# Fewer products in a linear-attention backward pass, and other buffers at the entrance of a softmax core

## Chip, cores and metric

One core of one Trainium2 chip. The metric is the device time of one execution in microseconds (us), lower is better. The kernel before takes 1096.92 us (median of 3 runs, 1093.32 to 1097.35). All runs told here are of the fast state; differences are called faster or slower only above 2%, so most of what follows is about effects below that line, and rests on profiles and on many runs.

Engines have the profiler's names: PE is TensorE's matrix products, PEld its weight loads, ACT is ScalarE, DVE VectorE, POOL GpSimd, SP SyncE; a q behind a name (SPq) marks the issue of a transfer. The granted clock is the share of TensorE's full clock that a throttle let through; a run's "clock" is its mean over the run.

## The reference, cut to what matters

Forward and backward (a vector-Jacobian product) of two attention blocks on 2048 tokens of 448 features with 16 heads of 28: A is linear attention, B is softmax attention with one shared k and v.

```python
phi = lambda t: jnp.where(t > 0, t + 1, jnp.exp(t)) + 1e-6
kv  = einsum("bhsd,bhse->bhde", phi(k), v);  z = einsum("bhsd->bhd", phi(k))
o_A = einsum("bhqd,bhde->bhqe", phi(q), kv) / (einsum("bhqd,bhd->bhq", phi(q), z) + 1e-6)
o_B = softmax(q k^T / sqrt(28)) v          # k, v shared by the 16 heads
out = concat([o_A @ wo_A, o_B @ wo_B]);    # returned with the gradients of all inputs
```

## The kernel before

It has three stages: A (linear attention, to about 200 us), the projections of B (to about 228 us), and the core of B, a loop of 512 units, each of two 128x512 tiles of scores, with its backward part 16 units behind (so "unit 16" is the first in which all engines work). The parts that matter:

```python
# awk: ring of 3 buffers per name. "osb" serves the outputs of A and the spread 1/den alike
def den_rx(q4, todo):
    for s in todo:
        rx = awk.tile([P, 512], BF16, name="osb")[:, 0:D]
        nc.scalar.activation(out=rx..., in_=rden[:, st, :]...to_broadcast([P, H, DH]), func=ACT.Copy)
        nc.vector.tensor_tensor(out=pq[:, st, 0:D], in0=pq[:, st, 0:D], in1=rx, op=ALU.mult)
        nc.vector.tensor_tensor(out=wq_n[:, st, 0:D], in0=wq_n[:, st, 0:D], in1=rx, op=ALU.mult)
def outA(st):
    ...                                        # 4 products into ps
    ot = awk.tile([P, 512], BF16, name="osb")[:, 0:D]
    nc.scalar.activation(out=ot[:], in_=ps[:, :], func=ACT.Copy)
    nc.scalar.dma_start(out0[st * P:(st + 1) * P, 0:D], ot[:])
# ... gradient of x of A: 3 x 4 products for each of the 16 token tiles
for st in range(NS):
    for tT_, w_ in [(pkT, VWT), (gqT, wqT), (gkT, wkT)]:
        for k in range(4):
            mm(ps[:, :], tT_[:, st, k, :], w_[:, k, :], start=(n == 0), stop=(n == 11))
# ... B: q by tokens (qn, 16 KB of each partition) is made by DMA transposes and written to memory
nc.sync.dma_start(qn_d[q2, :].rearrange(...), qn[:, t2, :])          # two writes of 1 MB
# v and k by tokens: 128 products of 32 columns
for w, dst in [(1, vaug_), (0, kn_)]:
    for st in range(NS):
        for c in range(4):
            mm(ps[:, st, :], xbT[:, c, st * P:(st + 1) * P], rep[:, w, c, 0:32], ...)
    nc.vector.tensor_copy(out=dst, in_=ps[:])
# core: the pools are stacked on memory that stage A and qn used
px_ = tile_pool(name="cdsx", bufs=2); pq_ = tile_pool(name="cqX", bufs=2)
pc_ = tile_pool(name="ccp", bufs=3);  pw_ = tile_pool(name="cwk", bufs=4)
```

## Time and profile before

| window of the profile before (us) | what it is | PE busy | granted clock |
|---|---|---|---|
| 62 to 110 | A: its outputs and gradients by token tile | 45.6 of 48.0 | 1.00 |
| 110 to 224 | A's weight and input gradients, B's projections | 113.8 of 114.0 | 1.00 |
| 224 to 229 | border to the core | 4.0 of 5.0 | 1.00 |
| 229 to 243 | entrance of the core, PE at half clock | 13.5 of 14.0 | 0.51 |
| 254 to 1047 | core | 758 of 793 | 1.00 |

The lines behind this table are in the prediction. Three more lines are needed later: rl (the reciprocals of the softmax sums, the core's first small tile) and the load of qX (q for the core), both behind the second write of q, and the first product with the backward scores, where unit 16 begins (timeline of the kernel before; columns: start, length, engine, line, operation, out<-in, shape, count; in brackets the idle time before it and what ended it).

```profile
246.59 0.18 DVE L762 RECIPROCAL rl<-sps 128x4 f32<-128x4 f32 x1 [0.86 <-DMA qn_d<-gaT]
247.08 1.16 POOL L878 DMA_DIRECT2D qX<-qn_d  x2 [18.66 <-PE dps L80]
254.08 0.69 DVE L870 TENSOR_TENSOR dsT<-dps,eT 128x512 bf16<-128x512 f32 x1
```

### The profile page before, as it was taken

The numbers are of one execution on the slowest core, as the hardware profiler recorded it, in microseconds if no ns is written. First come the engines' busy times: TensorE is split into PE (matmuls) and PEld (weight loads), VectorE is DVE, ScalarE is ACT, GpSimd is POOL, SyncE is SP. The second block draws the span as 40 slices with busy tenths as digits, with TensorE's granted clock in tenths as the row PEclk, the third lists the DMA queues.
The fourth block names the chain that finished last, engine by engine and source line by source line (L and its number), as shares of the span: only waits on it lengthen the run. The fifth ranks groups of instructions, "written<-read, shape, count | busy, mean of one in ns | idle before, by whom it ended". The sixth has DMA issues, their size and how long they took to land.

```text
span 1093.6 us, 38651 instructions
## 1 busy us (share of the span) xinstructions
PE 1047.3 (96%) x15645; PEld 489.8 (45%) x15645; DVE 896.3 (82%) x1772; ACT 876.1 (80%) x1744; POOL 758.1 (69%) x986
## 2 busy tenths in 40 slices
PE   9999999999999999999999999999999999999998
PEld 5545555444444444444444444444444444444444
DVE  7887400427999999999999999999999999999842
ACT  6453122468999999999999999999999999999521
POOL 6001242226888888888888888988988898888740
PEclk9999999979999999999999999999999999999999
DMA  9969899299999999999999999999999999999962
GB/s 264 153 126 173 172 173 213 61 200 224 183 209 173 174 190 187 197 181 192 196 179 195 193 196 185 196 196 172 198 192 196 185 193 188 192 180 178 221 139 63
DMA packets 668338, 198.96 MB, mean 182 GB/s; under 512 B 645392, under 2 KB 664128, under 8 KB 668160
## 3 DMA queue, kind: packets, MB, share of 16 engines
q1 hardware_dynamic: 656320, 175.18, 93.6%
q0 software_dynamic: 6880, 17.37, 6.3%
q10 hardware_dynamic: 4960, 3.96, 1.3%
q8 instruction: 122, 2.00, 0.7%
q14 instruction: 56, 0.46, 0.1%
HBM read 21.00 MB, written 12.94 MB: 31 GB/s over the span
## 4 chain that ended last, share of the span: by engine, by line
PE 35%; POOL 26%; ACT 23%; issue 10%; DVE 3%; DMA 1%; POOLq 0%; ACTq 0%; DVEq 0%
POOL dsT L873 22%; ACT cp L872 13%; PE agen L80 13%; ACT eT L903 9%; PE aacc L80 5%; PE sps L80 4%; PE oq L633 4%; PE sps L633 3%; PE dps L80 2%; PE dv_acc L633 2%; PE dk_acc L633 1%; PE dps L633 1%; DMA out_dram<-osb 1%; POOL prod L767 1%; POOL don L770 1%
## 5 line engine op out<-in xcount | busy, mean ns | idle before, releaser
L873 POOL TENSOR_TENSOR dsT<-cp,eT 128x512 bf16<-128x512 bf16 x512 | 588.4, 1157 | 103.9 <-ACT cp L872 96.4
L934 DVE STREAM_TRANSPOSE dsx<-dsT 128x512 f32<-128x512 f32 x512 | 357.6, 699 | 2.0
L870 DVE TENSOR_TENSOR dsT<-dps,eT 128x512 bf16<-128x512 f32 x512 | 342.3, 668 | 16.5 <-PE dps L633 9.1
L865 ACT ACTIVATE eT<-sps 128x512 bf16<-128x512 f32 x512 | 312.5, 610 | 27.5 <-PE dps L633 12.9
L633 PEld LDWEIGHTS <-R 32*128 32x128 bf16 (+1 forms) x8192 | 203.1, 93 | 281.9 <-issue 254.4
L872 ACT ACTIVATE cp<-dps 128x512 bf16<-128x512 f32 x512 | 314.1, 614 | 11.6 <-PE dps L633 9.3
L903 ACT ACTIVATE eT<-sps 128x512 bf16<-128x512 f32 x512 | 320.3, 626 | 0.0
L633 PE MATMUL dk_acc<-dsx,qX 32*32 32x512 bf16 x4096 | 268.0, 375 | 0.0
L633 PE MATMUL dps<-doT,R 32*128 32x256 bf16 x2048 | 248.9, 269 | 12.9 <-DVE dsT L870 7.5
L633 PE MATMUL sps<-R,R 32*128 32x256 bf16 x2048 | 218.7, 275 | 2.6 <-DVE oTs L763 0.8
L633 PE MATMUL oq<-eT,R 128*32 128x256 bf16 x2048 | 158.5, 276 | 0.0
L633 PE MATMUL oq<-dsT,R 128*32 128x256 bf16 x2048 | 157.2, 275 | 0.1
L633 PEld LDWEIGHTS <-qX 32*32 32x32 bf16 x4096 | 79.7, 89 | 114.7 <-issue 53.9
L633 PE MATMUL dv_acc<-eN,don 128*32 128x512 bf16 x1024 | 108.7, 379 | 0.0
L80 PEld LDWEIGHTS <-R 128*128 128x128 bf16 (+1 forms) x673 | 57.6, 99 | 55.8 <-issue 24.8
L396 POOL MEMSET ga<- 64x448 bf16 x2 | 0.9, 472 | 94.4 <-DVE pr L347 81.4
L546 DVE TENSOR_TENSOR osb<-R 32x512 bf16<-32x512 bf16 x4 | 1.6, 412 | 62.3 <-ACT R L543 62.3
L633 PEld LDWEIGHTS <-don 128*32 128x32 bf16 x1024 | 33.8, 97 | 0.7 <-issue 0.2
L888 DVE TENSOR_SCALAR R<-oq 64x256 bf16<-64x256 f32 x64 | 27.3, 427 | 4.6 <-PE oq L633 2.6
L878 POOL DMA_DIRECT2D qX<-qn_d x32 | 18.1, 570 | 18.7 <-PE dps L80 18.7
L80 PE MATMUL agen<-R,R 128*128 128x448 bf16 x128 | 28.6, 352 | 0.5 <-DVE pq L234 0.3
L499 ACT ACTIVATE wdq<-agen 128x448 bf16<-128x448 f32 x16 | 8.7, 543 | 25.1 <-PE agen L80 25.1
(219 smaller groups left out, 1012.4 us busy)
## 6 DMA issues: line engine op xcount, KB each, us to landing
qX<-qn_d POOLq DMA_DIRECT2D x32, 256.0 KB, 4.6
out_dram<-osb ACTq DMA_DIRECT2D x22, 112.0 KB
qn_d<-gaT SPq DMA_DIRECT2D x2, 1024.0 KB
eN<-eT SPq DMA_TRANSPOSE x128
xa<-in_A_x_dram SPq DMA_DIRECT2D x8, 224.0 KB
ga<-in_grad_out_dram SPq DMA_DIRECT2D x4, 448.0 KB
xa<-in_grad_out_dram POOLq DMA_DIRECT2D x4, 448.0 KB, 8.8
out_dram<-wdq POOLq DMA_DIRECT2D x8, 224.0 KB, 4.5
```

The source lines that it names most:

```text
L80: nc.tensor.matmul(out_ap, lhsT=lhsT, rhs=rhs, start=start, stop=stop, tile_position=(0, 0))
L633: nc.tensor.matmul(out, lhsT=lhsT, rhs=rhs, start=start, stop=stop, tile_position=pos, skip_group_check=True)
L767: nc.gpsimd.tensor_tensor(out=prod[b][:], in0=dnv, in1=os_, op=ALU.mult)
L770: nc.gpsimd.tensor_tensor(out=dn[:], in0=dnv, in1=r_[:].to_broadcast([P, 2, 2, 32]), op=ALU.mult)
L865: nc.scalar.activation(out=eT(u)[:, 0, :], in_=sp[0][:, :], func=ACT.Exp, scale=scale)
L870: nc.vector.tensor_tensor(out=dst[:, 0, :], in0=dp[0][:, :], in1=ew[:, 0, :], op=ALU.mult)
L872: nc.scalar.activation(out=cp[:, :], in_=dp[1][:, :], func=ACT.Copy)
L873: nc.gpsimd.tensor_tensor(out=dst[:, 1, :], in0=cp[:, :], in1=ew[:, 1, :], op=ALU.mult)
L878: nc.gpsimd.dma_start(qX[qc][32 * a:32 * a + 32, :, :, :].rearrange("j b s c -> j b (s c)"), qn_d[qc * 256:(qc + 1) * 256, :].rearrange("( ...
L888: nc.vector.tensor_scalar(out=qT_B[g][64 * hp:64 * hp + 64, qc * 256:(qc + 1) * 256], in0=oq[64:128, 0:256], scalar1=scale, scalar2=None, ...
L903: nc.scalar.activation(out=eT(u)[:, 1, :], in_=sp[1][:, :], func=ACT.Exp, scale=scale)
L934: nc.vector.transpose(out=dsx[b][:, tp, :, :, :].rearrange("p h t c -> p (h t c)").bitcast(F32), in_=dsT[y][:, :, :].rearrange("p h c -> p ...
```

## The change

Four parts. (1) The spread 1/den leaves the ring "osb", which output transfers hold, for the ring "phiT". (2) The last 64 features of q's gradient are put into the unused half of pk's last chunk, so eleven products do what twelve did. (3) v and k by tokens are picked out of rows already projected, by a selection matrix: 32 narrow products for 128. (4) The core's pools are stacked in another order, to take its first tiles off the memory of q by tokens.

```diff
 # 1
-                rx = awk.tile([P, 512], BF16, name="osb")[:, 0:D]
+                rx = awk.tile([P, D], BF16, name="phiT")[:, :]
 # 2
         for q4 in range(4):
+            t4 = slice(4 * q4, 4 * q4 + 4)
+            nc.gpsimd.tensor_copy(out=pk[:, t4, D:512], in_=gqn[:, t4, 3 * P:D])
             dma_T(pkT, pk, 4 * q4, 4)
@@
         prod_to(VWT, dkvT_blk, wvT, False)
+        nc.gpsimd.dma_start(VWT[64:128, 3, :], wqT[0:64, 3, :])
@@
-            for tT_, w_ in [(pkT, VWT), (gqT, wqT), (gkT, wkT)]:
-                for k in range(4):
-                    mm(..., start=(n == 0), stop=(n == 11))
+            for tT_, w_, nk in [(pkT, VWT, 4), (gqT, wqT, 3), (gkT, wkT, 4)]:
+                for k in range(nk):
+                    mm(..., start=(n == 0), stop=(n == 10))
 # 3
+        sel = cA.tile([P, 32], BF16, name="sel")          # identity without its first row
@@
-        for w, dst in [(1, vaug_), (0, kn_)]:
+        for rows, dst in [(vT, vaug_), (kT, kn_)]:
             for st in range(NS):
-                for c in range(4):
-                    mm(ps[:, st, :], xbT[:, c, st * P:(st + 1) * P], rep[:, w, c, 0:32], ...)
+                mm(ps[:, st, :], rows[:, st * P:(st + 1) * P], sel[:, :])
 # 4
+        pqa_ = cs_.enter_context(tc.tile_pool(name="cqXa", bufs=1, side="right"))
         px_ = cs_.enter_context(tc.tile_pool(name="cdsx", bufs=2, side="right"))
-        pq_ = cs_.enter_context(tc.tile_pool(name="cqX", bufs=2, side="right"))
+        pqb_ = cs_.enter_context(tc.tile_pool(name="cqXb", bufs=1, side="right"))
@@
-        wo = pp_.tile([P, 4, D], BF16, name="wo", bufs=1)
+        wo = pc_.tile([P, 4, D], BF16, name="wo", bufs=1)
@@
-                        qX[qc] = pq_.tile([P, 4, 2, 512], BF16, name="qX")
+                        qX[qc] = (pqb_ if qc % 2 else pqa_).tile([P, 4, 2, 512], BF16, name="qX")
```

More of the change, by code (lines that the diff above doesn't have):

```diff
@@ L494, in phase_A @@
             n = 0
-            for tT_, w_ in [(pkT, VWT), (gqT, wqT), (gkT, wkT)]:
-                for k in range(4):
-                    mm(ps[:, :], tT_[:, st, k, :], w_[:, k, :], start=(n == 0), stop=(n == 11))
+            for tT_, w_, nk in [(pkT, VWT, 4), (gqT, wqT, 3), (gkT, wkT, 4)]:
+                for k in range(nk):
+                    mm(ps[:, :], tT_[:, st, k, :], w_[:, k, :], start=(n == 0), stop=(n == 10))
                     n += 1
@@ L524, in phase_B_pre @@
             nc.gpsimd.memset(neg[32 * j:32 * j + 1, :], -1.0)
+        sel = cA.tile([P, 32], BF16, name="sel")
+        nc.gpsimd.tensor_copy(out=sel[:], in_=identB[:, 0:32])
+        nc.gpsimd.memset(sel[0:1, :], 0.0)
         kmx = cA.tile([H, NQC], F32, name="kmx")
@@ L580, in phase_B_pre @@
                 nc.sync.dma_start(qn_d[q2, :].rearrange("(t p) c -> p t c", p=P), qn[:, t2, :])
-        for w, dst in [(1, vaug_), (0, kn_)]:
+        for rows, dst in [(vT, vaug_), (kT, kn_)]:
             ps = gen([P, NS, 32])
             for st in range(NS):
-                for c in range(4):
-                    mm(ps[:, st, :], xbT[:, c, st * P:(st + 1) * P], rep[:, w, c, 0:32], start=(c == 0), stop=(c == 3))
+                mm(ps[:, st, :], rows[:, st * P:(st + 1) * P], sel[:, :])
             nc.vector.tensor_copy(out=dst, in_=ps[:])
```

## The prediction

> **What bounds the kernel now.** First the page: its totals and the row of granted clock over 40 slices.
>
> ```profile
> span 1093.6 us, 38651 instructions
> PE 1047.3 (96%) x15645; PEld 489.8 (45%) x15645; DVE 896.3 (82%) x1772; ACT 876.1 (80%) x1744; POOL 758.1 (69%) x986
> DVE  7887400427999999999999999999999999999842
> POOL 6001242226888888888888888988988898888740
> PEclk9999999979999999999999999999999999999999
> ```
>
> DVE and POOL show two programs in one: linear attention up to about 225 us, where POOL does little, and the softmax core from about 254 us, where DVE, ACT and POOL are all near full. The clock row has one dip, in slice 8 (219 to 246 us). An average share tells nothing here, so I next cut the span at the borders of the stages (columns: window, its length, busy us of PE, PEld, DVE, ACT and POOL, granted clock, DMA share, GB/s).
>
> ```profile
> 78.00:81.00 3.00, 0.99 (x7) 0.40 (x5) 0.70 (x3) 0.84 (x2) 0.00 (x0) 1.00 1.27 212
> 81.00:110.00 29.00, 28.70 (x169) 14.70 (x167) 21.28 (x42) 11.53 (x27) 3.48 (x6) 1.00 0.89 170
> 110.00:224.00 114.00, 113.83 (x604) 56.26 (x602) 26.66 (x62) 34.45 (x62) 36.24 (x79) 1.00 0.81 153
> 224.00:229.00 5.00, 3.96 (x130) 3.37 (x127) 1.81 (x3) 2.43 (x5) 2.92 (x7) 1.00 0.77 152
> 229.00:243.00 14.00, 13.51 (x81) 5.30 (x82) 2.55 (x6) 8.39 (x16) 0.00 (x0) 0.51 1.14 236
> 243.00:254.00 11.00, 10.77 (x108) 5.34 (x108) 5.20 (x14) 8.40 (x18) 2.42 (x6) 1.00 1.13 224
> 254.00:1047.00 793.00, 758.34 (x13728) 342.48 (x13729) 760.28 (x1450) 759.34 (x1516) 685.80 (x812) 1.00 1.10 190
> ```
>
> From 110 to 224 us PE idles 0.17 of 114 us: a matmul taken out there shortens the kernel by its own length. The core takes 793 us, 72% of the span, and the diff leaves its instructions as they are. So whatever is gained must come from the first 254 us. Two places in the timeline there stand out. The first is a hole in PE inside the stage that makes the output of linear attention:
>
> ```profile
> 78.25 0.10 PEld L80 LDWEIGHTS <-pqpT 128*128 128x128 bf16 x1
> 79.69 0.58 ACT L320 ACTIVATE osb<-rden 128x448 bf16<-128x448 f32 x1 [2.34 <-DMA out_dram<-osb]
> 80.30 0.39 DVE L322 TENSOR_TENSOR pq<-pq,osb 128x448 bf16<-128x448 bf16 x1 [2.55 <-ACT osb L320]
> 80.61 0.92 PE L80 MATMUL agen<-KO,pqpT 128*128 128x448 bf16 x4 [2.01 <-ACT ddT L354]
> ```
>
> The ACT copy that spreads 1/den over a row (line 320) takes a buffer of the ring "osb", and all three are still being written out to memory. ACT runs in order, so the small ddT copy behind it waits too, and PE waits for that: 2.01 us. The second place is the border to the core:
>
> ```profile
> 224.83 2.68 PE L80 MATMUL agen<-K,pk 128*128 128x32 bf16 x101
> 225.03 0.68 ACT L572 ACTIVATE R<-aacc,kmax 16x512 bf16<-16x512 f32 x1 [0.92 <-PE aacc L80]
> 225.72 1.28 ACT L844 ACT_TABLE_LOAD   x1
> 227.02 0.20 ACT L844 ACTIVATE ex<-ex 128x1 f32<-128x1 f32 x1
> 227.54 0.69 DVE L586 CAST R<-agen 128x512 bf16<-128x512 f32 x1 [0.91 <-PE agen L80]
> 228.29 0.50 PE L633 MATMUL sps<-R,R 32*128 32x256 bf16 x5 [0.79 <-DVE R L586]
> 228.84 0.60 ACT L865 ACTIVATE eT<-sps 128x512 bf16<-128x512 f32 x1 [1.62 <-PE sps L633]
> ```
>
> The 128 small products (27 run before the last sum of squares, 101 here) make v and k by tokens. The core's first score matmul waits for the cast of their result, and ACT, ready since 227.22, waits for that.
>
> **What the Trainium skill says.** "TensorE: Matmul & The Clock Gate", section "Wait — 56ns, not 53.3ns?", puts a floor of about 25 ns on the distance of two matmuls however narrow they are. The trace agrees: the chain of waits has the 101 narrow products as 2.53 us, 25.0 ns each, so narrow products are paid by their number. The same page, "Back-to-back issue gap", has N/2.4 + 2.5 ns for one alone, 189 ns at N = 448; the chain has 64 products of that width in 12.21 us, 191 ns each. I use the 191. The same page, Part 1, says that the clock is halved after an idle window of about 3.4 us, and that the window runs freely. The trace shows a granted clock of 0.50 or 0.51 from about 229.3 to 242.9 us, after the narrow products and two short holes; that is 13.6 us, four such windows. "ScalarE: Activation LUTs", section "What ACT_TABLE_LOAD costs", measures 1283 ns for a table load; here it is 1.28 us, and it limits what the border can give.
>
> **The change part by part.**
>
> Part 1, the 1/den copies leave the ring "osb" for the ring "phiT". That ring is read only by DVE, within a microsecond, and never by a transfer. The 2.34 us wait of ACT goes, and with it PE's 2.01 us hole. The rest of 81 to 110 us has 0.30 us of PE idle, so nothing more is to be had: **2.0 us**. Beside it, three of the factor tiles that the scheduler had hoisted to about 51 us (0.27 us of DVE each, the same ring) move behind this stage in the changed program's order; PE was busy there, so I count nothing.
>
> Part 2, twelve products per token tile become eleven. The last chunk of q's gradient is put in the empty lower half of the last chunk of pk, and its weight rows in the empty half of VWT. It removes 16 products of 448 columns: 16 x 0.191 = **3.1 us**, all on saturated PE. It adds four POOL copies (128x256 elements, which I estimate at 0.3 to 1 us each, from the 0.55 us of the 128x448 copies on POOL) and one small transfer. POOL is busy 36 of 114 us there. These must be done before the transposes of pk, the last of which is issued at 117.78 us, while the stage that reads them is some 45 us later in the chain. I count no loss.
>
> Part 3, v and k by tokens are selected out of the rows already projected: 32 narrow products for 128. The changed program keeps 27 of them before the last sum of squares and puts 5 after. PE saves 96 x 25 ns = 2.4 us, but not all is on the path. The last sum of squares ends at 224.99 and five products later it is 225.15; the cast of v can run before that, the cast of k (0.69 us) ends at about 226.0, so PE could start the core at 226.0 instead of 228.29. ACT, however, has its square root until 225.7, the table load until 227.0 and the dummy exponential until 227.22. The first exponential thus moves from 228.84 to 227.25: **1.6 us**.
>
> Part 4, the core's buffers move. Going by the sizes of the pools, the memory of q by tokens lay under the two qX buffers, cp and the small work tiles; now it lies under the second dsx buffer, the second qX and wo, which are used later. Before, the small tile rl waited 0.86 us and the qX load on POOL came only at 247.08, both after the second write of q landed. But from 243 to 254 us PE idles only 0.23 us, and ACT is 76% busy, so these waits were mostly hidden: **0.2 us**.
>
> Sum: 2.0 + 3.1 + 1.6 + 0.2 = 6.9 us.
>
> **The rivals.** (a) The half-clock stretch goes or shrinks. In it two units of the core take 3.98 us (dps products at 231.57 and 235.55), after it 2.46 us (247.57 and 250.03). So 13.6 us hold 6.8 units, which at full clock take 8.4: its cost is 5.2 us. For it: the run of narrow products before the border shrinks from 3.2 to 0.8 us. Against it: PE's holes grow, since it now waits for the table load (estimate 2.2 us of idle between 225.2 and 227.9, against 1.5 before). Since the window runs freely, I give 3 in 10 that it mostly goes: 1085 instead of 1090.
>
> (b) The gain at the border is given back. The core's first 16 units need the second write of q (issued at 240.60) and the transposes of the exponentials, a queue that starts at 235.51 behind the transposes of q. If those set when unit 16 can start, the 1.6 and 0.2 us vanish: about 1092. For it speaks a DMA share above 1.1 from 229 us on; against it that PE has hardly any hole between 243 and 254 us.
>
> (c) The extra copies and the small transfer, in order on POOL ahead of the stores of q's weight gradient, hold up the ring "osb" and with it PE: then part 2 gives 1 instead of 3 us and the time is about 1092. The 9 us in which ACT is idle after those stores speak against it.
>
> (d) The new addresses in the core change how its engines collide. Over 512 units of 1.55 us a change of 0.5% would be 4 us either way. Nothing in the profile speaks for it; I only widen the range.
>
> **Range and chances.** From 1096.9, 6.9 us less is 1090.0; three tenths of the 5.2 us of rival (a) take it to 1088.5, and a tenth or two for (b) and (c) back to **1089**. The three runs before spread over 4 us, and the clock stretch is worth 5, so the range is **1084 to 1094**. A change of 2% would be 22 us, three times the sum, and nothing that I see could slow the core by that: faster 0.02, same 0.97, slower 0.01.
>
> **What would show it right or wrong.** Part 1: no PE hole of 2 us near 78 to 81 us, and no 1/den copy waiting for a transfer. Part 2: 240 - 16 products in the long stretch of PE before the border, still without idle. Part 3: the run of 128x32 products is 5 long after the last sum of squares, and the first exponential follows the dummy one within 0.1 us. Part 4: no small tile waits for the write of q. Then the core should start about 6.7 us earlier, at about 222.1 us, and take as long as before, apart from the clock. I am wrong if PE shows new waits between 110 and 220 us, if the length of the core changes by more than 2 us for another reason than the clock, or if the half-clock stretch changes and the time with it.

## The result, and the profile after

The changed kernel takes 1086.18 us (median of 4 runs, 1083.65 to 1087.94) against 1096.9 before: ratio 0.9908, 95% interval 0.9879 to 0.9936. A second series, in another call, gave 0.9902. By the 2% rule it is the same; it is clearly about 10.5 us less. (Ratios here are the mean time of one kernel's fast runs over that of the other's of the same rounds, so not quite the ratio of the medians quoted.)

The page of the changed kernel first; then its windows, cut to match those of before (columns as in the prediction).

```profile
span 1086.2 us, 38438 instructions
PE 1039.1 (96%) x15533; PEld 486.5 (45%) x15533; DVE 895.3 (82%) x1772; ACT 875.7 (81%) x1744; POOL 759.5 (70%) x993
PEclk9999999989999999999999999999999999999999
```

```profile
78.00:81.00 3.00, 3.00 (x17) 1.43 (x16) 3.00 (x8) 2.30 (x5) 0.00 (x0) 1.00 1.15 214
81.00:108.00 27.00, 25.33 (x153) 13.32 (x152) 19.89 (x42) 9.12 (x22) 5.09 (x10) 1.00 1.11 190
108.00:220.00 112.00, 111.89 (x586) 55.27 (x585) 26.57 (x62) 34.95 (x62) 35.80 (x79) 1.00 0.77 157
225.00:230.00 5.00, 5.00 (x32) 1.83 (x31) 1.27 (x3) 2.99 (x7) 0.00 (x0) 0.50 1.21 273
230.00:235.00 5.00, 5.00 (x44) 2.40 (x42) 1.27 (x3) 3.42 (x7) 1.16 (x2) 0.81 1.07 196
```

The hole at 78 to 81 us is gone, but 81 to 108 us now has 1.67 us of idle where the stretch before had 0.30. The half-clock stretch is half as long: 6.8 us (from 225.0 us on) instead of 13.6. The timeline shows the new hole; the transpose of pk in its first line is issued by SP, the store in its second by ACT.

```profile
88.83 3.47 SPq L92 DMA_TRANSPOSE pq<-pk  x1
96.06 0.35 ACTq L368 DMA_DIRECT2D out_dram<-osb  x1
96.46 0.27 ACT L354 ACTIVATE ddT<-agen 16x128 bf16<-16x128 bf16 x1 [2.28 <-DMA pq<-pk]
96.78 0.92 PE L80 MATMUL agen<-KO,pqpT 128*128 128x448 bf16 x4 [1.61 <-ACT ddT L354]
```

Again ACT stands still in order, and PE behind it for 1.61 us, but for another reason: not a buffer, but the store itself. In the trace the transfers of SP and ACT are counted on the same eight counters (semaphores), and this store has the one that that transpose had. The chain of waits follows the transpose for 7.15 us, from its issue to its landing, and the store is issued then. The Trainium skill, "DMA: Bandwidth & Descriptors", section "Anatomy of one DMA — SWDGE (gpsimd) path", says that a transfer's semaphore wait takes place on the sequencer that issues it; the trace agrees, since the small copy behind the store on ACT waits too, 2.28 us in all.

The border and the entrance of the core (timeline):

```profile
221.45 0.28 PE L80 MATMUL agen<-sel,R 128*128 128x32 bf16 x5
222.35 1.28 ACT L850 ACT_TABLE_LOAD   x1
222.52 0.50 PE L639 MATMUL sps<-R,R 32*128 32x256 bf16 x5 [0.79 <-DVE R L591]
223.75 0.58 ACT L871 ACTIVATE eT<-sps 128x512 bf16<-128x512 f32 x1
224.38 0.37 PE L639 MATMUL sps<-R,R 32*128 32x256 bf16 x3 [1.37 <-ACT eT L871]
230.08 1.16 POOL L884 DMA_DIRECT2D qX<-qn_d  x2 [5.23 <-PE sps L639]
239.69 0.46 SPq L586 DMA_DIRECT2D qn_d<-gaT  x1
246.66 0.69 DVE L876 TENSOR_TENSOR dsT<-dps,eT 128x512 bf16<-128x512 f32 x1 [0.27 <-PE dps L639]
```

Five narrow products are left after the last sum of squares, the first exponential follows the table load, and qX is loaded at 230.08, long before the second write of q (239.69) is even issued; before, it was loaded at 247.08, after that write. The two profiles add up from borders in their chains of waits and timelines (us):

| piece | before | after | difference |
|---|---|---|---|
| start to the first four-tile accumulation | 59.73 | 60.62 | +0.9 |
| from there to q's weight gradient (part 1) | 51.49 | 50.47 | -1.0 |
| on to the long run of PE | 50.30 | 50.08 | -0.2 |
| long run of PE: 240 and 224 products (part 2) | 47.47 | 44.45 | -3.0 |
| its end to the first exponential (part 3) | 19.85 | 18.13 | -1.7 |
| first exponential to unit 16 (part 4, clock) | 25.24 | 22.91 | -2.3 |
| unit 16 to the end | 839.52 | 839.54 | 0.0 |

This makes 7.4 us. (The first row is scatter: over all 14 profiles that point lies between 59.7 and 60.6 us, 60.6 in two profiles without parts 1 and 2 and 59.7 in c_no4.) The profile of before was of a run that is short for its kernel (1095.3 us) and that of after the longest of its four (1087.94 us), so over all runs there are about 3 us more. The experiments look for those, and for what each part does alone.

### The profile page after: what moved, and what is told of

The parts are those of the page before. It is cut to its first block, busy times and chain, and to the rows that moved or that the text cites. A ratio compares the mean times of both kernels' runs of the same rounds, so it can differ in the third digit from the quotient of the medians.

```text
span 1086.2 us, 38438 instructions
## 1 busy us (share of the span) xinstructions
PE 1039.1 (96%) x15533; PEld 486.5 (45%) x15533; DVE 895.3 (82%) x1772; ACT 875.7 (81%) x1744; POOL 759.5 (70%) x993
## 4 chain that ended last, share of the span: by engine, by line
PE 34%; POOL 28%; ACT 23%; issue 10%; DVE 3%; DMA 1%; POOLq 0%; ACTq 0%; SPq 0%; DVEq 0%
POOL dsT L879 24%; PE agen L80 13%; ACT cp L878 12%; ACT eT L909 8%; PE aacc L80 4%; PE sps L80 4%; PE oq L639 4%; PE sps L639 2%; PE dps L80 1%; PE dv_acc L639 1%; POOL prod L773 1%; PE dk_acc L639 1%; POOL don L776 1%; PE dps L639 1%; ACT eT L871 1%
## 5 line engine op out<-in xcount | busy, mean ns | idle before, releaser
L773 POOL TENSOR_TENSOR prod<-R,oTs 128x128 f32<-128x128 bf16 x64 | 27.7, 433 | 8.1 <-DVE oTs L769 8.1
L759 PE MATMUL sps<-identF,oTs 64*128 64x64 f32 x128 | 21.4, 247 | 7.5
```

The lines of the kernel that those rows point to most:

```text
L759: nc.tensor.transpose(onp[:, qb, :, :].rearrange("p h c -> p (h c)"), oTs[0:64, qb * P:(qb + 1) * P], identF[0:64, 0:64], tile_position=(0 ...
L773: nc.gpsimd.tensor_tensor(out=prod[b][:], in0=dnv, in1=os_, op=ALU.mult)
```

## The experiments

Twelve kernels ran in three calls; the kernel before was run many times beside them, 61 times for the first four, 28 for the next four and 16 for the last four. Each edit is given against the kernel it starts from.

**a1_ring**: the kernel before with diff 1 alone.

```diff
-rx = awk.tile([P, 512], BF16, name="osb")[:, 0:D]
+rx = awk.tile([P, D], BF16, name="phiT")[:, :]
```

> The kernel before with part 1 alone (the 1/den copies in the ring phiT). Theory: the 2.0 us hole of PE near 78 to 81 us goes, and the stage from the first four-tile accumulation (59.73 us before) to the accumulation of q's weight gradient (111.22) shrinks from 51.5 us to 49.5. Rival: another wait takes its place, a store of the outputs that ACT can only issue once an earlier transfer on its counter has landed (in the changed kernel one such wait of ACT is 2.3 us long); then the stage is 50.5 us or longer, with or without the other parts. Time: 0 to 2 us less, within the scatter of the runs.

Ratio 0.9966 (0.9952 to 0.9979), 18 runs, so 3.7 us less. In its profile the stage takes 48.87 us, 2.6 less, with no wait for a transfer and a single wait of PE, of 0.3 us. So the first theory holds here. (At the entrance of the core this profile gains nothing: rl waits 2.87 us for the write of q, PE stands for 1.85 us, and unit 16 begins at 254.07, where it began before.) Over all profiles of this study that have part 1 the stage took 48.87, 48.93, 49.19, 50.47, 50.54, 50.55, 52.79 and 52.99 us (mean 50.5, stores on ACT); in the five without it 51.37, 51.49, 51.53, 52.19 and 53.25 us (mean 52.0). The five with part 1 above 50 us all show a wait of ACT for a transpose of pk; the three below do not. So the rival is right too, in some profiles: **programs with part 1 spend 1.4 us less here on average**, and up to 2.6. The longest three stages of all (52.79, 52.99 and 53.25 us) each hold, besides a hole of PE of 2.1 to 2.4 us, a stretch of 3.4 us at half clock right behind it.

But the other seven with part 1 have part 2 as well, whose copies must come before the transposes of pk. In a1_ring the first two of these are issued (timeline)

```profile
71.54 3.34 SPq L92 DMA_TRANSPOSE pq<-pk  x1
81.65 2.45 SPq L92 DMA_TRANSPOSE pq<-pk  x1
```

and in the changed kernel at 79.48 and 88.83 us, behind two other transposes, the second now on the counter that the store at 96 us needs. Of the nine profiles with part 2 and stores on ACT, seven show ACT waiting for a transpose between 95 and 101 us; of the four without part 2, none. So it is most likely part 2 that takes back what part 1 gives. With one profile of part 1 without part 2, this is not shown.

**a2_fold**: the kernel before with diff 2 alone.

```diff
+nc.gpsimd.tensor_copy(out=pk[:, t4, D:512], in_=gqn[:, t4, 3 * P:D])
+nc.gpsimd.dma_start(VWT[64:128, 3, :], wqT[0:64, 3, :])
-for tT_, w_ in [...]:  for k in range(4)
+for tT_, w_, nk in [(pkT, VWT, 4), (gqT, wqT, 3), (gkT, wkT, 4)]:  for k in range(nk)
```

> The kernel before with part 2 alone (eleven products for twelve). Theory: the long run of PE before the last projections of q holds 224 products instead of 240 and is 3.0 us shorter (44.5 instead of 47.5 us), PE without idle there; the hole of 2.0 us at 78 to 81 us stays, since the ring is the old one. Rival: the copies into pk delay the transposes of pk and with them the stores of ACT, so that the stage before (51.5 us) gets 1 to 2 us longer and the net gain is 1 to 2 us.

The long run of PE has 224 products in 44.45 us, 3.0 less, as said. The stage of part 1 takes 51.53 us, no longer than before; but in it PE's hole behind the ring is 1.1 us instead of 2.0, and a second one of 0.75 us has come, behind a transpose, so the rival may be right in part. Yet the time is only 0.9986 (0.9974 to 0.9998), 1.5 us. The rest is lost where the next two experiments look: in its profile rl waits 2.47 us for the write of q, and PE stands for 1.45 us.

**a3_sel**: the kernel before with diff 3 alone.

```diff
-mm(ps[:, st, :], xbT[:, c, st * P:(st + 1) * P], rep[:, w, c, 0:32], ...)   # x4
+mm(ps[:, st, :], rows[:, st * P:(st + 1) * P], sel[:, :])
```

> The kernel before with part 3 alone (32 narrow products for 128). Theory: the last sum of squares stays where it was, the first exponential of the core comes 1.6 to 1.7 us earlier relative to it (2.5 instead of 4.2 us after its start), limited by the table load of ACT. The stretch at half clock after the border: theory that the narrow products count as idle says it shrinks from 13.6 us to 6.8 or nothing; rival that it is the phase of a free-running window says it is of any length between 0 and 14 us whatever the part, and differs between runs of one kernel as much as between kernels.

The first exponential comes 18.22 us after the long run of PE instead of 19.85: 1.6 us earlier, as expected. And the time does not move: 0.9998 (0.9981 to 1.0015). In its profile the half-clock stretch at the border is only 3.4 us, PE runs ahead, and then stands for 5.2 us, because rl waits 6.21 us for the second write of q; during that hole the clock falls to half again, for 13.6 us. What part 3 gains is lost whole at this gate, as I call such a wait from here on.

**a4_mem**: the kernel before with diff 4 alone.

```diff
-pq_ = tile_pool(name="cqX", bufs=2)
+pqa_ = tile_pool(name="cqXa", bufs=1)   # ahead of cdsx
+pqb_ = tile_pool(name="cqXb", bufs=1)   # behind it; wo from cout to ccp
```

> The kernel before with part 4 alone (buffers of the core moved). Theory: the waits of rl and of the qX load for the write of q go, the load is issued several us earlier, but PE, which had 0.2 us of idle in the first 11 us of full clock, gains at most 0.3 us; the core from its unit 16 to the end takes the 839.5 us that it took before. Rival: the moved addresses change the speed of the core by 2 us or more.

0.9968 (0.9953 to 0.9983), 3.5 us, and not the 0.3 at most that was expected. Its profile shows the load of qX at 235.93, before the second write of q is issued at 244.91, and 839.1 us from unit 16 to the end, as before: in this profile the speed of the core is untouched, so that rival falls here. Its profile fell in a run with the long half-clock stretch (13.6 us), where nothing is gained. The runs say when something is. Grouped by granted clock (mean us, number of runs, all of this call; three runs of before below 0.992 are left out):

| granted clock | 0.992 | 0.993 | 0.994 | 0.995 | 0.996 | 0.997 | 0.998 |
|---|---|---|---|---|---|---|---|
| before | 1100.1 (13) | 1096.5 (8) | 1096.8 (4) | 1096.3 (24) | 1096.3 (2) | 1096.0 (7) | - |
| part 4 alone | 1097.6 (1) | 1094.9 (1) | 1098.8 (2) | 1095.1 (6) | 1093.8 (3) | 1092.5 (2) | 1091.5 (5) |

Before, from 0.993 to 0.997 the time does not follow the clock, which fits a start of the core that is set by the write of q and not by the half-clock stretch. With part 4, the time falls with it. This is a hint and no proof: the mean clock also counts half clock elsewhere, the step of 3.6 us at 0.992 is not explained, and no profile shows the kernel before with a short stretch. I read it as a gate, which c_no4 below tests, and which was hidden in the one profile I had read because that profile had a long stretch at half clock, behind which the gate just vanished (0.86 us of wait of rl, none of PE).

**b0_after**: the changed kernel unaltered.

> The changed kernel unaltered, as the reference on the same chip for the other three, and for the spread of its granted clock over many runs. Theory (free-running window): its runs fall in groups of clock (0.992 to 0.998), and, since part 4 took the wait for the write of q off the entrance of the core, its time follows the clock at about 0.5 us per us of half clock, where the kernel before follows it at less than 0.4. Ratio to before 0.99.

0.9902 (0.9879 to 0.9926), 6 runs, mean 1086.2 us; clock 0.995 in three (1087.6 us) and 0.997 in three (1084.8). Two groups, and the time seems to follow. But the profiled run (0.995, 1090.5 us) is long for other reasons, and without it the groups are only 1.4 us apart. It has 3.4 us of half clock at the border; as much in the stage of part 1, which takes 52.79 us, with a wait of PE of 2.2 us behind the transpose of pk; and as much again at 319 us, where PE waits 1.67 us for a transpose eN that the core itself issued.

**c_no4**: the changed kernel without diff 4.

```diff
-pqa_ / px_ / pqb_ ; wo in ccp
+px_ = tile_pool(name="cdsx", bufs=2); pq_ = tile_pool(name="cqX", bufs=2) ; wo in cout
```

> The changed kernel without part 4: parts 1, 2 and 3 on the old buffers of the core. Theory: what parts 1 to 3 gain before the core is lost at its entrance, because the small tile rl then waits 3 to 6 us for the second write of q, PE stands still behind it for 2 to 5 us and falls to half clock again; unit 16 of the core starts about as late as in the kernel before with the same inputs landing, and the time is 3 to 6 us above the changed kernel, 1089 to 1093. Rival (my prediction): part 4 is worth 0.2 us, so the time is within 1 us of the changed kernel.

0.9967 (0.9956 to 0.9978), 22 runs, mean 1093.2 us, 7.0 us above b0_after of the same call (give or take 3 us, by the two intervals). Parts 1 to 3 alone give 3.6 us where they should give 6. Its timeline:

```profile
237.47 0.46 SPq L586 DMA_DIRECT2D qn_d<-gaT  x1
242.64 0.18 DVE L767 RECIPROCAL rl<-sps 128x4 f32<-128x4 f32 x1 [5.73 <-DMA qn_d<-gaT]
242.86 0.29 DVE L768 TENSOR_TENSOR oTs<-sps,rl 128x128 f32<-128x128 f32 x1
243.20 0.61 PE L638 MATMUL sps<-R,R 32*128 32x256 bf16 x4 [4.70 <-DVE oTs L768]
```

and its windows:

```profile
223.00:229.00 6.00, 5.43 (x31) 2.09 (x30) 0.85 (x2) 4.02 (x9) 1.04 (x2) 0.50 0.91 239
229.00:239.00 10.00, 9.39 (x91) 4.74 (x91) 3.39 (x8) 7.52 (x15) 0.00 (x0) 0.98 1.19 192
239.00:243.00 4.00, 0.00 (x0) 0.00 (x0) 0.33 (x2) 0.00 (x0) 0.00 (x0) 0.58 1.06 287
243.00:253.00 10.00, 9.80 (x63) 3.81 (x62) 2.66 (x8) 5.22 (x10) 2.46 (x6) 0.50 1.14 211
```

The write lands, rl and oTs follow, and PE starts in that moment after 4.70 us of nothing; the hole throttles the clock and the next ten microseconds run at half. Unit 16 begins at 253.58, within 0.5 us of the kernel before, although the first exponential was 5.9 us earlier (222.94 against 228.84). This gate moves with the last square root of the projections: in the five profiles on the old buffers rl came 20.5 to 22.4 us after the start of the table load, which follows that square root at once. Parts 1 and 2 move the square root and so can carry through in part (in a1_ring's profile they do not); part 3 moves only the first scores and gives nothing without part 4. My rival is refuted.

**b2_warm**: the changed kernel with needless work in PE's two holes at the border.

```diff
+for _ in range(3):   # before the first scores;  and 6 more after unit 0's scores
+    nc.tensor.matmul(dv_acc[:, :], lhsT=identB[:, :], rhs=R2x[:, 1, :], start=True, stop=True, ...)
```

> The changed kernel with nine needless 512-column products where PE waits at the border (three before the first scores, six after them; into a bank of PSUM that is not in use yet). Theory: the stretch at half clock comes from those two holes of PE (0.8 and 1.4 us); filled with 9 x 0.22 us of work it does not come at all in most runs, the mean clock is 0.998 or more, and the time is 2 to 4 us less, 1082 to 1085. Rival: the clock falls for another reason (the small share of the array that the core's first products use), then the stretch is as long as in the changed kernel and the time is the same or up to 0.5 us more.

Its profile shows no throttling at all:

```profile
span 1082.0 us, 38449 instructions
PEclk9999999999999999999999999999999999999999
```

First exponential to unit 16 took 20.95 us, against 22.91 with 6.8 us of half clock, 21.67 with 3.4 us (b0_after) and 25.50 with 13.6 us (a4_mem): a us of half clock costs 0.2 to 0.33 us here. Work in the two holes, 0.8 and 1.4 us, keeps half clock away from this place, in this profile and in that of d2_late_warm; the twelve without it all have it there. But only five of the seven runs have 0.997 or more; two fell to 0.992 and 0.993 and took 1094.1 and 1092.8 us. The mean, 1087.8 us, is no better than the changed kernel's 1086.2 (ratio to before 0.9917, 0.9888 to 0.9946). As a remedy it fails.

**b3_store**: the changed kernel with the stores of A's output issued by POOL.

```diff
-nc.scalar.dma_start(out0[st * P:(st + 1) * P, 0:D], ot[:])
+nc.gpsimd.dma_start(out0[st * P:(st + 1) * P, 0:D], ot[:])
```

> The changed kernel with the 16 stores of the output of linear attention issued by POOL instead of ACT. Theory: the wait of ACT at 96 us, for an earlier transfer (a transpose of pk) to land before the next store can be issued, was what took back 1.6 us of the 2.0 to 2.6 us that part 1 gives alone; with the stores on POOL, ACT does not wait, PE has no hole of 1.6 us, and the stage from the first four-tile accumulation to that of q's weight gradient takes 48.9 us instead of 50.5: 1.5 us less in all. Rival: POOL, which also copies into pk, now waits for stores and delays the transposes; the stage is as long as in the changed kernel or longer.

The stage takes 49.36 us, without a wait of ACT for a transfer, as the theory says. The time does not follow: 0.9932 (0.9908 to 0.9955), mean 1089.3 us of six runs, 3 us above b0_after, though the two intervals overlap. In its profile unit 16 to the end takes 841.2 us, but in b0_after's it takes 841.6, so that does not tell them apart. Whether it is slower, and why, is open; it is no improvement.

**d1_late**: the changed kernel, with the core's buffers moved once more. In the kernel before, both qX, cp and the upper part of the pool of small tiles (whose first tile is rl) lay on the memory of q by tokens; in the changed kernel cp, the first dsx and the second qX still do. (These places are read off the built program, which is not kept in the record; b2_warm's profile bears out cp, which waits 0.3 us for the write of q there.) Here only the second dsx, the second qX and wo do (diff cut to the pools).

```diff
+pc_ = tile_pool(name="ccp", bufs=3)      # moved ahead
-px_ = tile_pool(name="cdsx", bufs=2)
+pxa_ = tile_pool(name="cdsxa", bufs=1); pxb_ = tile_pool(name="cdsxb", bufs=1)
+pwo_ = tile_pool(name="cwo", bufs=1)
```

> The changed kernel with its core's buffers moved once more, so that on the memory of q by tokens lie only tiles first used from unit 26 on (the second dsx buffer, the second qX, wo); in the changed kernel the three cp buffers (unit 16) and the first dsx (unit 18) still lie there. Theory: in its profile the second write of q no longer ends any wait of a tile; where the half-clock stretch is long nothing changes, where it is short 0.3 to 2 us are won: time 0 to 1 us below the changed kernel's 1085.5 to 1086.2. Rival: unit 16 does not come before the write has landed anyway, so it is the same.

0.9917 (0.9893 to 0.9941), six runs; no tile of the core waits for the write of q in its profile, but none did in the changed kernel's either. No gain is to be seen: the rival stands. The profile settles no more, since its core takes 844.0 us, 4.4 more than the changed kernel's, with two holes of PE, 1.3 and 2.7 us, at 296 and 306 us.

**d2_late_warm**: d1_late with the needless products of b2_warm.

> The same together with the nine needless products in the holes of PE at the border. Theory: the runs of the warm kernel that fell to a clock of 0.992 did so because PE, at full clock, reached unit 16 before the second write of q had landed, stood still for cp, and was throttled there; with cp elsewhere all runs stay at 0.997 or above and the time is 1081 to 1084. Rival: the low runs have another cause (the phase of the window, an earlier stage), then some still fall to 0.992 and the mean stays at 1086 to 1088.

Four of eleven runs have a clock of 1.000 and a mean of 1083.9 us, but two fall to 0.992 with 1097.7 us. Ratio 0.992 (0.989 to 0.995). So the wait for cp was not the cause of the low runs, and the theory falls. No profile caught such a run, so their cause stays open.

**b1_narrow**: the changed kernel with three needless narrow products beside each of the 32.

```diff
+for _ in range(3):
+    mm(ps[:, st, :], rows[:, st * P:(st + 1) * P], sel[:, :])
```

> The changed kernel with 96 needless narrow products at the border, 128 as in the kernel before. Theory: PE pays their number, 96 x 25 ns = 2.4 us, and the first exponential comes 1.6 us later, as it did before the change: 1.6 us more than the changed kernel. If narrow products count as idle for the clock, the mean clock also falls from 0.996 to 0.994 and the time rises by 3 to 4 us in all; if not, the clock is as in the changed kernel or better, since the holes of PE are smaller.

0.9928 (0.9911 to 0.9945), mean 1089.5 us, 3.3 us above b0_after (on another chip; 2.9 us by the ratios, whose intervals overlap). The first exponential waits 1.62 us for scores again, to the hundredth what it waited before the change. The half-clock stretch at the border is about 10 us in its profile, and the mean clock 0.9947, against 0.9960 in b0_after. This is what was expected if narrow products count as idle; but part 4 alone, which keeps the 128 narrow products, has a mean clock of 0.9957 over 20 runs, so the evidence is weak. I leave it open.

**e_no1**: the changed kernel without diff 1.

> The changed kernel without part 1: the 1/den copies again in the ring of the outputs. Theory: both waits of ACT are there, the one for a buffer (2.3 us near 78 us) and perhaps one for an earlier transfer on the store's counter; the stage is 51.4 us or longer against 50.5 and 52.8 in the two profiles of the changed kernel; 1 to 3 us more time than the changed kernel. Rival: the waits for transfers move about with the transfers so much that part 1 is not to be seen in the time (less than 1 us).

0.9929 (0.9910 to 0.9948), mean 1089.6 us, 3.4 us above b0_after (another chip again; 3.0 us by the ratios, whose intervals overlap). Its stage takes 52.19 us and shows the wait for a buffer (1.4 us) and two for transfers. This agrees with a1_ring on 3 to 4 us of time for part 1, while the stages give 1.4 to 2.6. The difference of about 1.5 us, within the noise, is not explained.

## Why the prediction was right, and where it was not

The time was right: 1089 in a range of 1084 to 1094, measured 1086.2. The gain was forecast as 7.9 us and was 10.7. That the profiles' 7.4 us came so near the 6.9 of the sum is partly luck: part 1 gave 1.0 instead of 2.0, and part 4 together with the clock 2.3 instead of 0.2. The first exponential came 5.1 us earlier, not 6.7. Step by step:

- **Part 1**, 2.0 us: the mechanism is shown (hole gone, a1_ring at -2.6 us). "Nothing more is to be had" was right, but a wait of the same kind came in its place in most profiles, through the counters of transfers, which I had not looked at. In the stage, 1.4 us on average.
- **Part 2**, 3.1 us: shown, 3.0 in each profile that has it, PE without idle around it. The copies took 0.40 us each, within the estimate. "I count no loss" was too kind, though: they put the transposes of pk later, and part 1's stage takes 50.8 us on average in the seven profiles with both parts, against 48.87 in a1_ring.
- **Part 3**, 1.6 us: shown at the border, 1.6 to 1.7. That it needs part 4 to reach the end of the kernel was not in my text. (A slip without effect: five products of 25 ns after 224.99 end at 225.12, not 225.15.)
- **Part 4**, 0.2 us: **this is the term that was mis-sized.** It measures 3.5 us alone and 7.0 us beside the other parts. The step that failed is "these waits were mostly hidden". They were hidden in that profile only, behind 13.6 us of half clock; in the four other profiles on the old buffers PE stands still for 1.45 to 5.19 us behind rl. I had both facts on the page and took each as fixed: I asked what rival (b) would give back in the changed kernel, and not whether the same gate already held up the kernel before whenever its clock was better. The list of what now lies on q's memory also left out cp and the first dsx (see d1_late).
- **Rival (a)**, the clock: its cost was put at 5.2 us; at 0.33 us for each, 13.6 us cost 4.5. The stretch did become shorter in the profile (6.8 us), which my text named as a sign of being wrong, and the mean granted clock rose from 0.994 (105 runs before) to 0.996 (10 runs after). At least part of that is part 4 again, since the hole behind the write of q throttles too (c_no4: 0.992).
- **Rival (b)** was the right mechanism in the wrong kernel. **Rival (c)** was wrong where I put it: PE's idle from 108 to 220 us is 0.11 us; what the copies cost came earlier. **Rival (d)** did not show in the pair (839.5 us from unit 16 in both) and is not settled: in three of the nine profiles on the moved buffers (b0_after, b3_store, d1_late) the core takes 841.2 to 844.0 us, with holes of PE of 1.3 to 2.7 us far inside it, in all others 838.5 to 840.1. That may be chance; no experiment tests it.

## What to carry to other kernels

A wait that costs nothing in a profile may be hidden by something that is not there in every run; before it is written off, ask what would end the stretch if the thing that hides it were gone, and compare times of many runs by their clock: a time that does not follow the clock may be held by something else, which putting the wait back will tell (c_no4). Where memory is reused from stage to stage, put on the bytes of the last transfer those tiles that are used last. And freeing a ring of buffers does not free the engine that issues the transfers: its next issue may wait for a transfer of another kind, and a copy that is cheap by itself can move such a transfer into its way.

## What the Trainium skill lacked or had wrong

- "TensorE: Matmul & The Clock Gate", Part 1, has the clock come back after at least one busy window of about 3.4 us, some 4 us into steady work. Here PE was busy without a gap and stayed at half for four such windows before (13.40 of 13.40 us busy from 229.5 to 242.9 us, clock 0.50) and for two in the changed kernel (6.80 of 6.80 us from 225.0 to 231.8). What decides the number is not shown.
- The same page, "HAM oscillation — how this bites in real kernels", warns of PE holes above about 3.4 us. Here holes of 0.8 and 1.4 us within 3 us came before half clock, and work put in them kept it away (b2_warm, 1.00 throughout in its profile); in the stage of part 1 single holes of 2.1 to 2.4 us came before half clock too, in three profiles of three, and those of 2.0 us or less did not.
- The same page, "Terms", puts the penalty of half clock at half of its time. In a stretch bound by several engines it was 0.21 to 0.33 us for each us: 20.95, 21.67, 22.91 and 25.50 us with 0, 3.4, 6.8 and 13.6 us of it.
- "DMA: Bandwidth & Descriptors" does not say that a transfer of one engine may be held up by one of another engine through a shared counter: 2.28 us of ACT behind a transpose issued by SP.
- "ScalarE: Activation LUTs", section "What ACT_TABLE_LOAD costs", adds about 1.38 us of drain to the 1.28 us load. Here the load began 0.02 us after the square root ended (222.33 us), and the dummy exponential began 0.01 us after the load ended (223.64 us); only the 1.28 us were paid.
